# Sparse attention and a hardswish MLP on one core: filler matmuls and a new order in the first batch

## The chip, the cores and the metric

The kernel runs on one core of a Trainium2 chip. A time is the device time of one execution in microseconds (us). A core has a matrix engine (TensorE, PE in the profile; PEld is its weight load), a vector engine (VectorE, DVE), a scalar engine (ScalarE, ACT), GpSimd (POOL) and the sync engine (SyncE, SP), which here only starts transfers. Each engine works through its own instruction queue in order; semaphores tie the queues together.

## The reference

Four batches of eight heads, 768 positions of 64 dimensions. Each query sees the keys less than 16 positions away, and one summary per block of 32 keys: the maximum of k over the block stands for its keys, the mean of v for its values.

```
k_sum = k.reshape(B, H, nb, block, D).max(axis=3)
v_sum = v.reshape(B, H, nb, block, D).mean(axis=3)
scores_l = where(|i - j| < 16, scale * q k^T, -1e9)
scores_s = scale * q k_sum^T + log(block)
a = softmax(concat(scores_l, scores_s))
x = a @ concat(v, v_sum)            # heads side by side: 3072 x 512
h = x @ w_in                        # 512 x 2048
out = (h * clip(h + 3, 0, 6) / 6) @ w_out
```

Inputs are float32 in HBM; the kernel computes in bfloat16 with float32 accumulation.

## The kernel before

Heads go in pairs, four per batch, so that two heads of 64 dimensions fill 128 partitions. For batch 0 the steps are, by the names in the code:

- `K(0, p)` transposes k of a pair on PE into PSUM (line 297), copies it into the block-diagonal `kbd` (line 306; ACT one half, then DVE the other), and takes block maxima `red` and `kst` on DVE (lines 310 and 317).
- `Tq(0, p, part)` transposes q on PE (line 336) and ACT copies it to `qT` (line 337). Part 0 has the first 480 positions, part 1 the rest.
- `Sl`, called for batch 0 by `S_first`, makes the local scores `sl` (line 345), ACT their exponentials `at` (line 348), DVE the mask (line 349). `Ss` makes the scores against summaries, `ss` to `asum`, for two pairs.
- `vsum0(p)` sums v over blocks with a matmul against indicators (`vps`, line 259). After the second pair of a group, ACT copies the sums (`vs`, line 263) and two small transfers bring them into the tile `vs96` (line 266); `to_vst` spreads them on DVE.
- `vcast(p)` writes v in bfloat16 into the block-diagonal `vbd` (line 248; ACT one half, DVE the other). Its off-diagonal parts must be zero first (line 205).
- `AV(0, p, half)` accumulates outputs `num` and softmax sums `den` on PE (lines 381 to 397), ACT forms 1/den as exp(-ln den) (lines 399 and 400), DVE multiplies into `x` (line 401).
- `F1(t, ft)` multiplies a tile of 384 rows of x by a 128-column piece of `win` (line 414, tile `hp`, four matmuls), then hardswish on ACT and DVE (lines 417 and 418). It needs x of all four pairs. `F2` multiplies by `wout` (line 431).

The part for the first half of batch 0 stands under a manual schedule: the order of the calls is the order on PE, ACT and DVE. After it, `F1` and `F2` for eight row tiles run as a list, and the remaining attention work is placed in slots between them by `plan`. F1 of row tile 0 is first; `Tq(0, 0, 1)` comes after its fourth piece at the latest.

Loads: SP brings v in float32 (`vf`). GpSimd starts all others, with a cast to bfloat16: k and q of batch 0 first, then two copies named `pace` (`hold_loads`) that wait for `vs96` of the second group, and after them, in `load_weights`, w_in parts 0 and 1, the second part of q, w_in parts 2 and 3, and four parts of w_out. GpSimd is in order, so nothing is issued before the copies are done.

PSUM pools `ps_h`, `ps_o` and `ps_s` have two buffers, and `ps_n` has one each under the tags `num` and `den`. `AV` takes its two tiles in turn from `ps_o` (where `alt` is true) and `ps_n`.

Of the kernel before, what the change touches and what calls it, by code (L numbers as in the profile page):

```python
# [9 lines left out]
F32 = mybir.dt.float32  # L10
BF16 = mybir.dt.bfloat16
# [5 lines left out]
D = 64  # L17
BLK = 32
KB = 64
HALO = 15  # L20
# [12 lines left out]
def kernel(  # L33
# [9 lines left out]
    nc = tc.nc  # L43
    B, H, S, _ = q.shape
    NP = H // 2
    NB = S // BLK
    NT = S // 128
    NK = S // KB
# [93 lines left out]
    def load_w_in(c):  # L142
        w = d_ff // 4
        nc.gpsimd.dma_start(out=w_in_sb[:, :, c * w:(c + 1) * w], in_=w_in_v[:, :, c * w:(c + 1) * w])
# [34 lines left out]
    def hold_loads(src):  # L179

        nc.gpsimd.tensor_copy(pace[0:src.shape[0], 0:1], src)
# [8 lines left out]
                            channel_multiplier=-1, pattern=[[NB, 4], [0, D]])  # L190
    hmv = [hm4[:, 2 * par:2 * par + 2] for par in range(2)]
    osum = [osum4[:, 2 * par:2 * par + 2] for par in range(2)]
    obd = const.tile([128, 2, D], BF16, tag="obd", name="obd")
    hmk = const.tile([128, 2, NB], BF16, tag="hmk", name="hmk")
    half_c = const.tile([128, 1], F32, tag="half", name="half_c")
    zero = const.tile([128, 1], F32, tag="zero", name="zero")
    nc.vector.memset(zero[:], 0.0)

    def zero_off_diagonal(eng, t):
        w = t.rearrange("p n c -> p (n c)").bitcast(F32).rearrange("p (n c) -> p n c", c=64)  # L200
        for r, c in ((slice(0, 64), slice(32, 64)), (slice(64, 128), slice(0, 32))):
            if eng is nc.scalar:
                eng.copy(w[r, :, c], zero[r].unsqueeze(2).to_broadcast([64, NK, 32]))
            else:
                eng.memset(w[r, :, c], 0.0)
# [24 lines left out]
    def to_vst(g, a):  # L230
        for par in range(2):
            nc.vector.tensor_tensor(vst[2 * g + par][:], a.unsqueeze(1).to_broadcast([RS, 2, D]), hmv[par],
                                    op=ALU.mult)
# [11 lines left out]
    def vcast(p):  # L245
        for j in range(2):
            rows = slice(64 * j, 64 * j + 64)
            (nc.vector.tensor_copy if j else nc.scalar.copy)(vbd[p][rows, :, rows], vf[p][rows])


    vps, vs96 = {}, {}

    def vsum0(p):
        g, par = p // 2, p % 2
        if par == 0:
            vps[g] = ps_n.tile([128, NK, D // 2], F32, tag=("num", "den")[g], name="vps")
        for h in range(2):
            c = 2 * h + par
            nc.tensor.matmul(vps[g][32 * c:32 * c + 32], ind[:], vf[p][:, :, h * (D // 2):(h + 1) * (D // 2)],  # L259
                             start=True, stop=True)  # L260
        if par == 1:
            a = ld.tile([128, NK, D // 2], F32, tag="vr", name="vs8", bufs=2)
            nc.scalar.copy(a[:], vps[g][:])  # L263
            vs96[g] = work.tile([RS, D], F32, tag="vs96", name="vs96")
            for h in range(2):
                (nc.sync if g == 1 and h == 0 else nc.gpsimd).dma_start(
                    out=vs96[g][:, h * (D // 2):(h + 1) * (D // 2)], in_=a[64 * h:64 * h + 64:8])


# [51 lines left out]
            nc.vector.tensor_tensor(o, red[:].unsqueeze(1).to_broadcast([128, 2, NB]), hmk[:], op=ALU.mult)  # L321

    def Tq(b, p, part=None):
        pool, tag = (ps_h, "h") if b == 0 else (ps_s, "s")
        tp = pool.tile([128, S], BF16, tag=tag, name="tp")
        t, i = qb_t[b, p, part]
        if b >= NLONG:
            for s in range(NT):
                nc.tensor.transpose(tp[:, s * 128:(s + 1) * 128], t[:, s].rearrange("p h d -> p (h d)"), ident[:])
            nc.vector.tensor_copy(qT[p][:, PAD:PAD + S], tp[:])  # L330
            return
        lo, hi, n = cut(part)
        r = (hi - lo) // n
        for s in range(n):
            for j in range(2):
                nc.tensor.transpose(tp[64 * j:64 * j + 64, s * r:(s + 1) * r], t[:, 2 * i + j, s], ident[0:r, 0:r])
        nc.scalar.copy(qT[p][:, PAD + lo:PAD + hi].rearrange("p (c s) -> p c s", s=n),
                       tp[:, 0:hi - lo].rearrange("p (s c) -> p c s", s=n))
# [12 lines left out]
    def Ss(b, g, half):  # L351
        sp = ps_s.tile([128, 512], F32, tag="s", name="ss")
        for par in range(2):
            p = 2 * g + par
            nc.tensor.matmul(sp[0:RS, 0:HALF], kst[p][:], qT[p][:, PAD + half * HALF:PAD + (half + 1) * HALF],  # L355
                             start=(par == 0), stop=(par == 1))
        a = work.tile([RS, HALF], BF16, tag="asum", name="asum", bufs=4)
        nc.scalar.activation(a[:], sp[0:RS, 0:HALF], AF.Exp, scale=scl)
        asum[b, g, half] = a
# [8 lines left out]
        return res  # L368

    xt = {}  # L370

    def AV(b, p, half):
        s = 2 * b + half
        if s not in xt:
            xt[s] = xp.tile([128, NP, HALF], BF16, tag="x", name="x")
        a, asm = at[p], asum[b, p // 2, half]
        alt = b == 0 and p % 2 == half
        pool = ps_o if alt else ps_n
        num = pool.tile([128, HALF], F32, tag="o" if alt else "num", name="num")
        bl = blocks_of(half)  # L380
        nc.tensor.matmul(num[:], vst[p][:].rearrange("p h d -> p (h d)"), asm[:], start=True, stop=False)  # L381
        for i, (t, lo, hi, off) in enumerate(bl):
            nc.tensor.matmul(num[:, lo:hi], vbd[p][:, t], a[:, t, off:off + hi - lo],  # L383
                             start=False, stop=(i == len(bl) - 1))
        den = pool.tile([128, HALF], F32, tag="o" if alt else "den", name="den")
        ones = obd[:].rearrange("p h d -> p (h d)")
        nc.tensor.matmul(den[:], osum[p % 2].rearrange("p h d -> p (h d)"), asm[:], start=True, stop=False)  # L387
        t0, t1 = (0, NK // 2) if half == 0 else (NK // 2, NK)
        d3 = den[:].rearrange("p (n c) -> p n c", c=KB)
        nc.tensor.matmul(d3, ones, a[:, t0:t1, HALO:HALO + KB], start=False, stop=False)  # L390

        if half == 0:
            nc.tensor.matmul(d3[:, :, KB - HALO:], ones, a[:, 1:7, 0:HALO], start=False, stop=False)
            nc.tensor.matmul(d3[:, 1:, 0:HALO], ones, a[:, 0:5, HALO + KB:], start=False, stop=True)  # L394
        else:
            nc.tensor.matmul(d3[:, 0:5, KB - HALO:], ones, a[:, 7:12, 0:HALO], start=False, stop=False)
            nc.tensor.matmul(d3[:, :, 0:HALO], ones, a[:, 5:11, HALO + KB:], start=False, stop=True)
        lg = work.tile([128, HALF], F32, tag="lg", name="lg")
        nc.scalar.activation(lg[:], den[:], AF.Ln)  # L399
        nc.scalar.activation(lg[:], lg[:], AF.Exp, scale=-1.0)  # L400
        nc.vector.tensor_tensor(xt[s][:, p], num[:], lg[:], op=ALU.mult)  # L401
# [55 lines left out]


    def load_weights():
        for c in range(2):  # L460
            load_w_in(c)
        load_q(0, 0, 4, 1)
        for c in range(2, 4):
            load_w_in(c)
        for c in range(4):
            load_w_out(c)

    def S_first(p):
        for lo, hi in ((0, 4), (4, NK0)):
            Sl(0, p, lo, hi)  # L470

    def v_first(p):
        vsum0(p)
        vcast(p)
        if p == NP - 1:
            hold_loads(vs96[1][:, 0:1])
            hold_loads(vs96[1][:, D // 2:D // 2 + 1])
            load_weights()

    zero_rest()  # L480
    K(0, 0)
    Tq(0, 0, 0)
    v_first(0)
    for p in range(2, NP):
        zero_off_diagonal(nc.vector, vbd[p])
    S_first(0)
    v_first(1)
    K(0, 1)
    Tq(0, 1, 0)
    S_first(1)  # L490
    nc.vector.tensor_scalar_mul(osum4[:], hm4[:], float(BLK))
    K(0, 2)
    to_vst(0, vs96[0][:])
    Tq(0, 2, 0)
    Ss(0, 0, 0)
    v_first(2)
    v_first(3)
    AV(0, 0, 0)
    K(0, 3)
    Tq(0, 3, 0)  # L500
    S_first(2)
    AV(0, 1, 0)
    S_first(3)
    Ss(0, 1, 0)
    to_vst(1, vs96[1][:])
    AV(0, 2, 0)
    AV(0, 3, 0)
    start.__exit__(None, None, None)

# [56 lines left out]
                 + [(None, NTILE - 1)])  # L566
    for n, (f1, f2) in enumerate(work_list):
        for i in range(NFT):
            if f1 is not None:
                F1(f1, i, f2 is None)  # L570
            if f2 is not None:
                for j in range(3):
                    F2(f2, 3 * i + j, by_ft=f2 == 0)
            for _, f in sorted(plan.pop(16 * n + i, []), key=lambda e: e[0]):
                f()
# [31 lines left out]
```

## Time and profile before

The median of three runs is 261.19 us (261.11 to 261.37). The profiled execution has a span of 259.2 us.

| engine | busy, us | share of the span |
|---|---|---|
| PE | 238.8 | 92% |
| ACT | 167.9 | 65% |
| DVE | 155.0 | 60% |
| GpSimd | 67.4 | 26% |

| stretch, us | PE busy | DVE busy | ACT busy | DMA share |
|---|---|---|---|---|
| 0 to 5 | 0.00 | 2.86 | 4.12 | 0.62 |
| 5 to 10 | 3.57 | 2.75 | 3.77 | 1.21 |
| 10 to 15 | 2.84 | 3.52 | 2.78 | 1.24 |
| 15 to 20 | 4.31 | 4.43 | 3.71 | 0.30 |
| 20 to 25 | 4.98 | 3.15 | 3.55 | 0.14 |
| 25 to 30 | 3.42 | 2.73 | 2.17 | 1.19 |
| 30 to 35 | 4.51 | 1.11 | 2.54 | 1.24 |
| 35 to 40 | 4.29 | 3.69 | 4.44 | 1.23 |

The first column of numbers is how long PE was busy in each stretch of 5 us; the last is the mean share of time in which the 16 DMA engines had work (over 1 where packets overlap). Transfers stop between about 16 and 23 us and then run without a pause; the PE has gaps until about 36 us and few after.

### The profile page before, as it was taken

What the parts mean: (1) busy time and instruction counts of PE and PEld (TensorE: products, weight loads), DVE (VectorE), ACT (ScalarE), POOL (GpSimd) and SP (SyncE); (2) the same over time, 40 slices, a digit from 0 to 9 for tenths busy, and PEclk for the clock granted to TensorE, in tenths of its full rate; (3) what the DMA queues carried; (4) which work ended last, traced back from release to release, by engine and by line L of the source; (5) the groups of instructions that cost most, each with busy time, mean ns of one, the idle gap of its engine ahead of it and who ended that gap; (6) DMA issues with size and microseconds to landing.
All of it is one profiled execution on the core that took longest, in us unless ns stands there. A gap on an engine that the chain in (4) does not pass through costs nothing.

```text
span 259.2 us, 5011 instructions
## 1 busy us (share of the span) xinstructions
PE 238.8 (92%) x1928; PEld 139.3 (54%) x1952; DVE 155.0 (60%) x357; ACT 167.9 (65%) x326; POOL 67.4 (26%) x101
## 2 busy tenths in 40 slices
PE   1779789999999999898999999999999999999994
PEld 1336446544555656565655555666655555555553
DVE  4877266622678938999884697657544444444400
ACT  8576479733887879868676656766856655555410
POOL 7316500842893103879330400000000000000000
PEclk9999999999999999999999999999999999999999
DMA  7962999999999185999991641101011111101122
GB/s 136 197 113 33 204 204 200 149 225 214 176 188 130 57 229 73 105 82 197 168 134 41 42 61 42 43 1 43 0 40 43 40 40 43 40 0 42 43 81 81
DMA packets 62847, 25.80 MB, mean 100 GB/s; under 512 B 51280, under 2 KB 58728, under 8 KB 62824
## 3 DMA queue, kind: packets, MB, share of 16 engines
q0 software_dynamic: 52848, 17.61, 58.8%
q1 hardware_dynamic: 9976, 7.88, 9.9%
q8 instruction: 15, 0.25, 0.4%
q14 instruction: 8, 0.07, 0.1%
HBM read 31.98 MB, written 6.29 MB: 148 GB/s over the span
## 4 chain that ended last, share of the span: by engine, by line
PE 73%; DVE 11%; DMA 6%; ACT 5%; issue 2%; SPq 1%; POOL 0%; ACTq 0%
PE op L431 28%; PE hp L414 27%; DMA vf<-in_v_dram 3%; PE sl L345 3%; DVE g L418 3%; PE num L383 3%; DMA win<-in_moe_w_in_dram 2%; PE ss L355 2%; PE num L381 2%; PE den L387 2%; PE den L390 2%; DVE red L312 1%; ACT r L417 1%; DVE x L401 1%; PE vps L259 1%
## 5 line engine op out<-in xcount | busy, mean ns | idle before, releaser
L414 PE MATMUL hp<-x,win 128*128 128x384 bf16 x512 | 105.4, 328 | 2.8 <-DVE g L418 1.5
L417 ACT ACTIVATE r<-hp,half_c 128x384 f32<-128x384 f32 x128 | 73.4, 580 | 45.4 <-PE hp L414 41.9
L418 DVE SCALAR_TENSOR_TENSOR g<-r,hp 128x384 bf16<-128x384 f32 x128 | 69.7, 551 | 51.5 <-ACT r L417 51.3
L431 PE MATMUL op<-wout,g 128*128 128x512 bf16 x344 | 93.6, 379 | 1.2 <-issue 0.3
L414 PEld LDWEIGHTS <-win 128*128 128x128 bf16 x512 | 47.4, 98 | 37.8 <-issue 5.6
L431 PEld LDWEIGHTS <-g 128*128 128x128 bf16 x368 | 35.2, 98 | 30.4 <-issue 0.6
L401 DVE TENSOR_TENSOR x<-num,lg 128x384 bf16<-128x384 f32 x32 | 17.7, 554 | 26.8 <-ACT lg L400 25.2
L399 ACT ACTIVATE lg<-den 128x384 f32<-128x384 f32 x32 | 15.7, 492 | 18.8 <-PE den L394 11.2
L120 POOL DMA_DIRECT2D vbd<-in_v_dram x24 | 18.1, 768 | 36.0 <-PE num L383 23.7
L348 ACT ACTIVATE at<-sl 128x376 bf16<-128x376 f32 (+2 forms) x48 | 22.2, 488 | 4.8 <-PE sl L345 4.7
L349 DVE TENSOR_TENSOR at<-at,mask 128x376 bf16<-128x376 bf16 (+2 forms) x48 | 16.3, 348 | 3.5 <-ACT at L348 3.2
L345 PEld LDWEIGHTS <-kbd 128*128 128x128 bf16 x192 | 12.5, 103 | 9.1 <-DVE kbd L306 1.8
L400 ACT ACTIVATE lg<-lg 128x384 f32<-128x384 f32 x32 | 16.8, 526 | 0.9
L345 PE MATMUL sl<-qT,kbd 128*128 128x94 bf16 x192 | 15.5, 216 | 1.7 <-DVE kbd L306 1.6
L435 ACT COPY ot<-op 128x512 f32<-128x512 f32 x23 | 13.2, 585 | 5.9 <-PE op L431 5.7
L383 PEld LDWEIGHTS <-vbd 128*128 128x128 bf16 x224 | 13.8, 103 | 5.6 <-issue 2.4
L383 PE MATMUL num<-at,vbd 128*128 128x94 bf16 (+2 forms) x224 | 14.9, 207 | 0.0
L113 POOL DMA_DIRECT2D qb<-in_q_dram x16 | 13.6, 882 | 4.1 <-PE hp L414 2.3
L113 POOL DMA_DIRECT2D kb<-in_k_dram x16 | 13.6, 874 | 0.4 <-PE hp L414 0.4
L381 PE MATMUL num<-asum,vst 96*128 96x384 bf16 x32 | 11.2, 350 | 0.8 <-ACT vs L263 0.6
L390 PE MATMUL den<-at,obd 128*128 128x384 bf16 x32 | 11.3, 352 | 0.0
L387 PE MATMUL den<-asum,osum 96*128 96x384 bf16 x32 | 10.9, 340 | 0.0
(87 smaller groups left out, 215.3 us busy)
## 6 DMA issues: line engine op xcount, KB each, us to landing
out_dram<-ot SPq DMA_DIRECT2D x23, 256.0 KB, 2.0
vr<-in_v_dram POOLq DMA_DIRECT2D x6, 768.0 KB, 9.4
vbd<-in_v_dram POOLq DMA_DIRECT2D x24, 96.0 KB, 3.7
win<-in_moe_w_in_dram POOLq DMA_DIRECT2D x4, 512.0 KB, 9.4
wout<-in_moe_w_out_dram POOLq DMA_DIRECT2D x4, 512.0 KB, 18.0
vf<-in_v_dram SPq DMA_DIRECT2D x8, 192.0 KB, 7.5
kb<-in_k_dram POOLq DMA_DIRECT2D x16, 96.0 KB, 5.0
qb<-in_q_dram POOLq DMA_DIRECT2D x16, 96.0 KB, 4.9
```

Source lines behind the costliest of these rows:

```text
L113: nc.gpsimd.dma_start(out=t[:, :, j], in_=src[b, 2 * p + j].rearrange("(s p) d -> p s d", p=128))
L120: nc.gpsimd.dma_start(out=vall[rows, p, lo:hi, rows], in_=v[b, 2 * p + j].rearrange("(n k) d -> k n d", k=KB)[:, lo:hi])
L345: nc.tensor.matmul(sp[:, i * WIN:(i + 1) * WIN], kbd[p][:, t], qT[p][:, PAD - HALO + t * KB:PAD - HALO + t * KB + WIN], start=True, stop=True)
L348: nc.scalar.activation(a, sp[:, 0:n * WIN].rearrange("p (n c) -> p n c", c=WIN), AF.Exp, scale=scl)
L383: nc.tensor.matmul(num[:, lo:hi], vbd[p][:, t], a[:, t, off:off + hi - lo], start=False, stop=(i == len(bl) - 1))
L390: nc.tensor.matmul(d3, ones, a[:, t0:t1, HALO:HALO + KB], start=False, stop=False)
L400: nc.scalar.activation(lg[:], lg[:], AF.Exp, scale=-1.0)
L401: nc.vector.tensor_tensor(xt[s][:, p], num[:], lg[:], op=ALU.mult)
L414: nc.tensor.matmul(hp[:], w_in_sb[:, kt, ft * 128:(ft + 1) * 128], xt[t][:, kt], start=(kt == 0), stop=(kt == NP - 1))
L417: nc.scalar.activation(r[:], hp[:], AF.Relu, bias=half_c[:], scale=1.0 / 6.0)
L418: last_g[0] = nc.vector.scalar_tensor_tensor(gt[t][:, ft], r[:], 1.0, hp[:], op0=ALU.min, op1=ALU.mult)
L431: nc.tensor.matmul(op[:], gt[t][:, ft, ts * 128:(ts + 1) * 128], w_out_sb[:, ft], start=(ft == 0), stop=(ft == NFT - 1))
```

## The change

It concerns the first half of batch 0 and the loads beside it.

- **Filler.** A tile `idle` of zeros is multiplied by itself in groups (`busy`, 33 matmuls of 512 columns in all) into PSUM tiles that nobody reads. Ten stand at the head of PE's queue, the others between the steps of the prologue. They are to keep the PE occupied while it waits.
- **Order.** K and Tq of pairs 2 and 3 come ahead of the first AV; scores of all four pairs too. `vcast` of pairs 2 and 3 moves behind the scores.
- **w_in part 0** is issued by itself as soon as v is in (a `pace` copy of the last v tile), not after the sums of v. The rest of `load_weights` still waits for them.
- **Zeros** of `vbd` for pairs 2 and 3 are written by GpSimd instead of DVE.
- **PSUM.** The filler holds `den` of `ps_n` and later a buffer of `ps_h`; `vps` always uses `num`; first parts of q are transposed into `ps_o`; in the first half AV takes `ps_o` for odd pairs instead of even ones.
- **Sums of group 1** go to `vs96` through SP alone.
- **F1 of row tile 0** may not be placed ahead of the end of AV(0, 2, 0).

```diff
+    for p in range(2, NP):
+        w = vbd[p].rearrange("p n c -> p (n c)").bitcast(F32).rearrange("p (n c) -> p n c", c=64)
+        nc.gpsimd.memset(w[0:64, :, 32:64], 0.0)
+        nc.gpsimd.memset(w[64:128, :, 0:32], 0.0)
...
+    nc.vector.memset(idle[:], 0.0)
...
+    def busy(t, n):
+        for _ in range(n):
+            nc.tensor.matmul(t[:], idle[:, 0:128], idle[:], start=True, stop=True)
+    busy_n = ps_n.tile([128, 512], F32, tag="den", name="busy_n")
+    busy(busy_n, 10)
...
-                (nc.sync if g == 1 and h == 0 else nc.gpsimd).dma_start(
+                (nc.sync if g == 1 else nc.gpsimd).dma_start(
...
-        pool, tag = (ps_h, "h") if b == 0 else (ps_s, "s")
+        pool, tag = (ps_s, "s") if b else (ps_o, "o") if part == 0 else (ps_h, "h")
...
-        alt = b == 0 and p % 2 == half
+        alt = b == 0 and p % 2 == 1
...
     zero_rest()
     K(0, 0)
+    busy(busy_n, 5)
     Tq(0, 0, 0)
-    v_first(0)
-    for p in range(2, NP):
-        zero_off_diagonal(nc.vector, vbd[p])
+    vsum0(0)
+    vcast(0)
+    K(0, 1)
+    busy(busy_n, 2)
     S_first(0)
-    v_first(1)
-    K(0, 1)
     Tq(0, 1, 0)
+    busy(busy_n, 3)
+    vsum0(1)
+    vcast(1)
+    nc.vector.tensor_scalar_mul(osum4[:], hm4[:], float(BLK))
+    busy(busy_n, 2)
+    K(0, 2)
     S_first(1)
-    nc.vector.tensor_scalar_mul(osum4[:], hm4[:], float(BLK))
-    K(0, 2)
-    to_vst(0, vs96[0][:])
+    busy(busy_n, 3)
     Tq(0, 2, 0)
-    Ss(0, 0, 0)
-    v_first(2)
-    v_first(3)
-    AV(0, 0, 0)
     K(0, 3)
     Tq(0, 3, 0)
+    busy(busy_n, 3)
+    Ss(0, 0, 0)
     S_first(2)
-    AV(0, 1, 0)
+    hold_loads(vf[NP - 1][:, 0, 0:1])
+    load_w_in(0)
+    vsum0(2)
+    vsum0(3)
+    for h in range(2):
+        hold_loads(vs96[1][:, h * (D // 2):h * (D // 2) + 1])
+    load_weights()
+    to_vst(0, vs96[0][:])
+    busy_h = ps_h.tile([128, 512], F32, tag="h", name="busy_h")
     S_first(3)
     Ss(0, 1, 0)
+    vcast(2)
+    busy(busy_h, 2)
     to_vst(1, vs96[1][:])
+    AV(0, 0, 0)
+    vcast(3)
+    AV(0, 1, 0)
+    busy(busy_h, 3)
     AV(0, 2, 0)
+    first_x = last_av[0]
     AV(0, 3, 0)
```

More of the change, by code (lines that the diff above doesn't have):

```diff
@@ L196 @@
     zero = const.tile([128, 1], F32, tag="zero", name="zero")
+    idle = const.tile([128, 512], BF16, tag="idle", name="idle")
+    nc.vector.memset(idle[:], 0.0)
     nc.vector.memset(zero[:], 0.0)
+    def busy(t, n):
[3 more added lines that the diff above has]
+    busy(busy_n, 10)
     def zero_off_diagonal(eng, t):
@@ L255, in vsum0 @@
         if par == 0:
-            vps[g] = ps_n.tile([128, NK, D // 2], F32, tag=("num", "den")[g], name="vps")
+            vps[g] = ps_n.tile([128, NK, D // 2], F32, tag="num", name="vps")
         for h in range(2):
@@ L370 @@
     xt = {}
+    last_av = [None]
     def AV(b, p, half):
@@ L393, in AV @@
             nc.tensor.matmul(d3[:, :, KB - HALO:], ones, a[:, 1:7, 0:HALO], start=False, stop=False)
-            nc.tensor.matmul(d3[:, 1:, 0:HALO], ones, a[:, 0:5, HALO + KB:], start=False, stop=True)
+            last_av[0] = nc.tensor.matmul(d3[:, 1:, 0:HALO], ones, a[:, 0:5, HALO + KB:], start=False, stop=True)
         else:
@@ L459, in load_weights @@
     def load_weights():
-        for c in range(2):
-            load_w_in(c)
+        load_w_in(1)
         load_q(0, 0, 4, 1)
@@ L470, in S_first @@
             Sl(0, p, lo, hi)
[L472 to L478, printed above, removed]
     zero_rest()
     K(0, 0)
+    busy(busy_n, 5)
     Tq(0, 0, 0)
-    v_first(0)
-    for p in range(2, NP):
-        zero_off_diagonal(nc.vector, vbd[p])
+    vsum0(0)
+    vcast(0)
+    K(0, 1)
+    busy(busy_n, 2)
     S_first(0)
-    v_first(1)
-    K(0, 1)
     Tq(0, 1, 0)
+    busy(busy_n, 3)
[4 more added lines that the diff above has]
+    K(0, 2)
     S_first(1)
-    nc.vector.tensor_scalar_mul(osum4[:], hm4[:], float(BLK))
-    K(0, 2)
-    to_vst(0, vs96[0][:])
+    busy(busy_n, 3)
     Tq(0, 2, 0)
-    Ss(0, 0, 0)
-    v_first(2)
-    v_first(3)
-    AV(0, 0, 0)
     K(0, 3)
     Tq(0, 3, 0)
+    busy(busy_n, 3)
+    Ss(0, 0, 0)
     S_first(2)
-    AV(0, 1, 0)
+    hold_loads(vf[NP - 1][:, 0, 0:1])
[7 more added lines that the diff above has]
+    busy_h = ps_h.tile([128, 512], F32, tag="h", name="busy_h")
     S_first(3)
     Ss(0, 1, 0)
+    vcast(2)
+    busy(busy_h, 2)
     to_vst(1, vs96[1][:])
+    AV(0, 0, 0)
+    vcast(3)
+    AV(0, 1, 0)
+    busy(busy_h, 3)
     AV(0, 2, 0)
+    first_x = last_av[0]
     AV(0, 3, 0)
@@ L568 @@
         for i in range(NFT):
-            if f1 is not None:
+            if f1 == 0:
+                with tc.issue_after(first_x.ins):
+                    F1(0, i, True)
+            elif f1 is not None:
                 F1(f1, i, f2 is None)
```

## The prediction

> **What bounds the kernel now.** I began with the page. TensorE (PE) is busy for 92% of 259.2 us, and the chain that ended last is 73% PE, so only stretches in which PE starves, or runs slowly, can give time back. The view of who waited for whom, for PE alone, puts them at the start:
>
> ```profile
> PE tp L297 <- DMA kb<-in_k_dram: 5.3, 1, 5.3
> PE sl L345 <- DVE kbd L306: 1.6, 1, 1.6
> PE hp L414 <- DVE g L418: 1.5, 2, 1.3
> ```
>
> The first two lie before 16 us, the longest of the third at 36 us. The chain, in order of time, gives what ended last there:
>
> ```profile
> 18.02 1.48 PE vps L259 x8
> 19.52 0.48 ACT vs L263
> 20.03 1.88 DMA vs<-vs
> 22.70 5.55 DMA win<-in_moe_w_in_dram
> 28.30 1.46 PE hp L414 x4
> 33.08 1.35 PE hp L414 x7
> ```
>
> The sums of v (vps, vs) hold back the first weights (win), and these hold the first F1 matmul (hp) until 28.30; from 33.08 the chain is almost all PE. Between lie the outputs of pairs 2 and 3, and the PE timeline shows at what speed they ran:
>
> ```profile
> 24.70 0.53 PE L390 MATMUL den<-at,obd 128*128 128x384 bf16 x1
> 28.30 1.46 PE L414 MATMUL hp<-x,win 128*128 128x384 bf16 x4 [0.62 <-DMA win<-in_moe_w_in_dram]
> 33.08 1.82 PE L414 MATMUL hp<-x,win 128*128 128x384 bf16 x10 [0.39 <-DVE x L401]
> 35.67 0.43 PE L336 MATMUL tp<-ident,qb 36*64 36x36 bf16 x16 [0.77 <-DVE g L418]
> 45.50 0.33 PE L390 MATMUL den<-at,obd 128*128 128x384 bf16 x1
> ```
>
> The same den matmul takes 0.53 us at 24.7 and 0.33 at 45.5; four hp take 1.46 us at 28.3, ten take 1.82 at 33.1. PE streams at half speed until about 31.3 us. The page's PEclk row reads 9 throughout, so that row doesn't show this state; durations do. The DMA view holds the third limit:
>
> ```profile
> win<-in_moe_w_in_dram POOLq DMA_DIRECT2D x1, 512.0 KB, 5.5
> qb<-in_q_dram POOLq DMA_DIRECT2D x1, 288.0 KB, 10.1
> ```
>
> Issued at 22.70, win part 0 lands at 28.2. Part 1, issued at 23.5, lands at 30.7. Then comes the second part of q (qb, issued at 24.28) at 34.4, win part 2 at 36.5, and the rest 2.5 us apart until 49.3.
>
> [...] 4 hp start 0.32 us apart before 31.3 and 0.16 after. [...]
>
> **The change, part by part.** Everything after F1(0)'s first 16 matmuls stands in the same order on every engine as before. So the effect is how much earlier that point is reached, here measured at the first transpose of q's second part (Tq(0,0,1), 35.67 before).
>
> *Products of zeros.* 33 matmuls of 512 columns. No row shows one at the slow clock. From hp's 0.32 us for 384 columns it is 0.43 (14.1 us in all); the op rows give 0.215 at the fast clock (7.1 us). I take fast from the second or third group on: the first ten and the next five run from 1.2 us (after a memset of about 0.2 us on DVE) with only K(0,0)'s 0.8 us block between[...]. If all 15 were slow, Tq(0,0,0) would come at 8.4 instead of 7.12; nothing pays, since K(0,1) waits for its k, which lands at 9.4 (3.33 + 6.1).
>
> *Zeroing vbd of pairs 2 and 3 on GpSimd.* Takes 1.87 us from DVE (10.05 to 11.92). On GpSimd it begins at 8.84; hm, 256 columns, takes 0.31 us there, so four of 384 columns are 0.5 each[...]: done by 12.9, when nothing is due.
>
> *K, Tq of pair 3 and the casts.* In the new order PE is at K(0,2) by 13.0, when its k has landed (4.66 + 8.2 = 12.9), and at Tq(0,2) for its q at 14.4 (5.34 + 9.1). ACT from the sums of pair 1 (12.6): vs 0.4, cast 0.7, kbd 0.7, exps 0.8, qT 0.5, kbd 0.7, qT 0.5, asum 0.5: 17.4. The second scores tile of pair 2 needs the buffer that asum frees, so vps of pairs 2 and 3 runs at 17.6 to 18.4 (half of 1.48) and the copy vs ends at 19.0.
>
> *DVE* from 14.7: kbd, red, kst of pair 2 2.2, mask 0.6, the same of pair 3 2.2, mask 0.6, vst 0.5: 20.8. There AV(0,0) starts. At the fast clock one AV takes 0.9 us (44.89 to 45.75 before). ACT now sets the pace from 20.7: cast 0.8, Ln and Exp 1.0, cast 0.8, three more Ln and Exp 3.0: 26.3, with small gaps 26.7. The last x is ready 0.6 later, at **27.3**, 5.7 us ahead of 33.04. Moving the casts here costs ACT 1.7 us behind AV, but takes the same from in front of it.
>
> *win part 0 early.* Its gate is now v itself. DMA share falls at 16.2, so issue at about 16.8 and landing at 22.3; it is off the path by 5 us. *The rest of the weights* still waits for the sums of pairs 2 and 3: copy at 19.0, two issues on SP of 0.75 each instead of one on SP and one on GpSimd, 1.9 to land: 22.4, with two gate copies and the issue gap 0.7 (21.96 to 22.70 before), of which half overlaps: win part 1 issues at 22.6, 0.9 us ahead. On a then idle queue it takes 5.5: 28.1. The second part of q lands 3.7 later, as before: **31.8**.
>
> *The sum.* F1(0) runs from 27.3; sixteen matmuls and the wait for g take 2.6 as before, so PE reaches Tq(0,0,1) at 29.9 and waits there until 31.8. PE is in order, so all of F1 is queued behind it. Gain 35.67 - 31.8 = 3.9 us: 261.19 - 3.9 = **257.3**. Later loads aren't short: win part 2 lands at 33.9, due at 36.6 or later; w_out part 0 at about 39, due at 46 (49.9 before).
>
> **Rivals.**
> A (forecast, 0.55): q's second part is the new bound, 257.3. Against it: its 3.7 us may shrink on queues that are less loaded; a lead of 0.5 us either way in the sums of v moves it one for one.
> B (0.25): q lands by 29.9, [...] because the sums land early. Then the last x bounds: gain 5.7, 255.5. Against: the trace's own 3.7.
> C (0.12): PE falls back to the slow clock, in the stall before Tq(0,0,1) or between the filler groups. [...] In the second four AV of 1.85 us take the place of 0.9 and the last x slips to 31: gain about 2, 259.2.
> D (0.08), slower: the clock never rises early. 14.1 us of filler and 20.4 us of PE work before 31.3 stand in one queue from 1.2 us, with at least 1 us of waits: the last output at 36.7 instead of 32.2, less what overlaps; some 3 us lost, 264. [...]
>
> **Numbers.** A, B and C are faster by over 0.2% (0.5 us); a few of the milder forms of D end near no change. Faster 0.91, same 0.02, slower 0.07. The range takes A with its half microsecond, B down to a further 0.3, C, and leaves D out: 255.2 to 259.4.
>
> **What would show it.** In the changed profile: den L405 at 0.33 us in AV(0,0) (clock); win part 0 landed near 22; the last x of batch 0 near 27.3; tp L350 of the 36-row form waiting 1 to 2 us for DMA qb; after it the same distances as before. Wrong would be: den at 0.53; no DMA wait at that transpose (B); or a gap in the later thirds of the span that wasn't there.

## The result and the profile after

The changed kernel takes 259.21 us (four runs, 258.93 to 259.65) where the kernel before takes 261.15 (260.16 to 261.37). The ratio is 0.9935, with a 95% interval from 0.9906 to 0.9963: faster by 1.9 us, half of the forecast 3.9. Measured again later beside other kernels it was 0.9924 (0.9896 to 0.9951).

The page of the kernel after, its span, its clock row and the F1 group, and below them the F1 group on the page of before:

```profile
span 257.4 us, 5112 instructions
PEclk9999799999999999999999999999999999999999
L429 PE MATMUL hp<-x,win 128*128 128x384 bf16 x512 | 105.6, 328 | 1.7 <-DVE g L433 1.5
L414 PE MATMUL hp<-x,win 128*128 128x384 bf16 x512 | 105.4, 328 | 2.8 <-DVE g L418 1.5
```

The span is 1.8 us shorter, the F1 matmuls cost what they cost before, and the clock row now has a dip in its fifth slice. The chain that ended last, in order of time (start, length, what), answers to that of before:

```profile
18.12 1.47 PE vps L273 x8
19.59 0.02 issue
19.62 0.48 ACT vs L277
20.09 0.03 ACT at L362
20.12 4.93 DMA vs<-vs
...
25.18 0.18 POOL pace L181
...
25.86 0.76 POOL win L144
26.62 7.26 DMA qb<-in_q_dram
33.88 0.04 issue
33.93 0.43 PE tp L350 x16
```

As forecast, w_in part 0 has left the chain and q's second part has taken its place. But the transfer of the sums, vs, takes 4.93 us where it took 1.88, so the rest of the weights goes out at 25.86 and not at 22.6. Both transfers were issued by 21.54. The packets of their queue, 208 in all, move only between 23.84 and 24.70, towards the end of those of w_in part 0, which was issued at 19.26 and landed at 24.98. The PE timeline shows the other thing that the late sums did:

```profile
21.89 0.34 PE L405 MATMUL den<-at,obd 128*128 128x384 bf16 x1
26.37 0.32 PE L396 MATMUL num<-asum,vst 96*128 96x384 bf16 x1 [2.56 <-DVE x L416]
28.75 0.53 PE L405 MATMUL den<-at,obd 128*128 128x384 bf16 x1
33.93 0.43 PE L350 MATMUL tp<-ident,qb 36*64 36x36 bf16 x16 [1.45 <-DMA qb<-in_q_dram]
```

The den matmul of the first pair runs in 0.34 us: the fast clock was there. The third output then waited 2.56 us (the row names x; DVE itself was held up by `vst`, which waited 3.45 us for the sums), and the den of the fourth pair takes 0.53 again. Busy time by stretch, whose third figure from the right is the granted clock, agrees:

```profile
27.00:28.00 1.00, 1.00 (x13) 0.80 (x12) 0.56 (x1) 0.55 (x2) 1.00 (x2) 0.73 0.47 18
28.00:29.00 1.00, 1.00 (x4) 0.45 (x3) 0.51 (x1) 0.46 (x1) 1.00 (x3) 0.50 0.93 145
```

**A yardstick.** In all 16 profiles the time from the start of the fourth transpose of q's second part to the end of the span is 217.1 to 217.5 us. Nothing behind that point matters; where it stands is the result. The first row is from before, the second from after:

```profile
42.03 0.43 PE L336 MATMUL tp<-ident,qb 36*64 36x36 bf16 x16
40.09 0.43 PE L350 MATMUL tp<-ident,qb 36*64 36x36 bf16 x16
```

That is 1.94 us earlier, the measured gain. (Of it, 1.74 us stand at the first transpose already.)

### The profile page after: what moved, and what is told of

Same layout as the page of the kernel before. It is cut to its first block, busy times and chain, and to the rows that moved or that the text cites. A ratio compares the mean times of both kernels' runs of the same rounds, so it can differ in the third digit from the quotient of the medians.

```text
span 257.4 us, 5112 instructions
## 1 busy us (share of the span) xinstructions
PE 243.7 (95%) x1985; PEld 139.3 (54%) x1985; DVE 154.2 (60%) x354; ACT 167.9 (65%) x326; POOL 69.2 (27%) x105
## 4 chain that ended last, share of the span: by engine, by line
PE 75%; DVE 10%; DMA 8%; ACT 3%; issue 2%; POOL 1%; DVEq 0%; POOLq 0%; ACTq 0%
PE op L446 29%; PE hp L429 26%; PE sl L359 3%; DMA qb<-in_q_dram 3%; PE num L398 3%; DMA kb<-in_k_dram 2%; DVE g L433 2%; DMA vs<-vs 2%; PE ss L369 2%; PE num L396 2%; PE den L402 2%; DVE red L326 1%; PE den L405 1%; PE tp L350 1%; PE busy_n L208 1%
## 5 line engine op out<-in xcount | busy, mean ns | idle before, releaser
L446 PE MATMUL op<-wout,g 128*128 128x512 bf16 x368 | 98.3, 379 | 0.0
L416 DVE TENSOR_TENSOR x<-num,lg 128x384 bf16<-128x384 f32 x32 | 17.8, 555 | 22.6 <-ACT lg L415 20.8
L362 ACT ACTIVATE at<-sl 128x376 bf16<-128x376 f32 (+2 forms) x48 | 22.4, 489 | 3.2 <-PE sl L359 3.1
L398 PEld LDWEIGHTS <-vbd 128*128 128x128 bf16 x224 | 13.0, 99 | 5.8 <-issue 2.3
L359 PEld LDWEIGHTS <-kbd 128*128 128x128 bf16 x192 | 11.9, 97 | 7.6 <-issue 2.2
L359 PE MATMUL sl<-qT,kbd 128*128 128x94 bf16 x192 | 14.5, 206 | 0.4 <-ACT asum L372 0.4
L398 PE MATMUL num<-at,vbd 128*128 128x94 bf16 (+2 forms) x224 | 14.3, 201 | 0.0
L396 PE MATMUL num<-asum,vst 96*128 96x384 bf16 x32 | 10.4, 326 | 2.6 <-DVE x L416 2.6
L208 PE MATMUL busy_n<-idle 128*128 128x512 bf16 x28 | 9.6, 482 | 1.3 <-DVE ind L223 1.3
```

The lines of the kernel that those rows point to most:

```text
L359: nc.tensor.matmul(sp[:, i * WIN:(i + 1) * WIN], kbd[p][:, t], qT[p][:, PAD - HALO + t * KB:PAD - HALO + t * KB + WIN], start=True, stop=True)
L362: nc.scalar.activation(a, sp[:, 0:n * WIN].rearrange("p (n c) -> p n c", c=WIN), AF.Exp, scale=scl)
L446: nc.tensor.matmul(op[:], gt[t][:, ft, ts * 128:(ts + 1) * 128], w_out_sb[:, ft], start=(ft == 0), stop=(ft == NFT - 1))
```

## The experiments

Single runs of one kernel can differ by over 3 us (e1: 258.5 to 262.1), so a kernel is judged by its ratio to runs of before that were measured beside it. The columns on the right, from one profile each, show where a kernel stands in the chain (us). A profile can be an extreme: that of e10 is the slowest of its 19 runs, that of e2 the slowest of six, that of e3 the second fastest of eleven. In the expectations, Q names the theory of the late sums and of what they hold back, C that of TensorE's clock; the first one defines both, and a third, S.

| kernel | ratio to before, 95% interval | last x done | first, fourth transpose |
|---|---|---|---|
| before | 1 | 34.0 | 35.67, 42.03 |
| changed | 0.9935 (0.9906 to 0.9963) | 31.1 | 33.93, 40.09 |
| changed, again | 0.9924 (0.9896 to 0.9951) | 31.3 | 33.41, 39.57 |
| e1 w_in part 0 after the sums | 0.9957 (0.9935 to 0.9979) | 27.3 | 35.60, 41.56 |
| e2 q ahead of w_in part 1 | 0.9887 (0.9860 to 0.9914) | 30.9 | 32.57, 39.98 |
| e3 no filler | 0.9931 (0.9904 to 0.9958) | 29.3 | 33.05, 39.05 |
| e4 more filler | 0.9955 (0.9934 to 0.9977) | 29.9 | 33.66, 41.45 |
| e5 sums issued with part 0 | 0.9889 (0.9857 to 0.9920) | 31.0 | 33.03, 39.19 |
| e6 no gate on the sums | 0.9990 (0.9972 to 1.0008) | 34.1 | 35.70, 42.06 |
| e7 before + early part 0 | 0.9914 (0.9881 to 0.9947) | 31.7 | 33.74, 40.00 |
| e8 before + filler | 1.0013 (0.9997 to 1.0029) | 34.4 | 36.10, 42.47 |
| e10 new order alone | 0.9953 (0.9934 to 0.9973) | 28.9 | 36.42, 42.39 |
| e11 e5 without filler | 0.9943 (0.9922 to 0.9965) | 29.7 | 33.20, 40.73 |
| e12 e11, one gate | 0.9870 (0.9831 to 0.9909) | 30.7 | 33.50, 39.76 |
| e13 sums not awaited | 0.9793 (0.9763 to 0.9823) | 27.8 | 30.23, 36.49 |
| e14 e13 without filler | 0.9792 (0.9766 to 0.9818) | 29.0 | 30.78, 37.04 |

**Why the sums came late: e1, e5, e6.**

```diff
-    hold_loads(vf[NP - 1][:, 0, 0:1])
-    load_w_in(0)
 def load_weights():
+        load_w_in(0)
         load_w_in(1)
```

> The changed kernel, with w_in part 0 issued after the sums of v again (no gate on v, part 0 heads the list before part 1). Theory Q (the small transfers of the sums land late, at 25.05, because they share the DMA engines with w_in part 0; everything issued after them, q's second part above all, then sets the end of F1's fourth piece): without part 0 beside them the sums land about 1.9 us after their second issue, near 22.7. Part 0 then lands near 28.6, part 1 near 31.1, q's second part near 34.8, so its first transpose is 0.9 us later than 33.93: about 260.1 us. Theory C (the gap of 2.6 us in TensorE before the third output and the slow clock after it cost the time): the sums at 22.7 remove gap and slow clock, the transpose comes near 31.2: about 256.5. Theory S (the sums land late because both are issued by SyncE, not because of part 0): they still land near 25, part 0 only near 31, q near 37: about 262.3.

Its chain of waits:

```profile
20.25 2.33 DMA vs<-vs
22.60 0.02 POOLq L181
22.70 0.30 POOL pace L181
23.18 5.39 DMA win<-in_moe_w_in_dram
```

With no load beside them the sums are there at 22.6, 2.3 us after the second issue, though both still go through SyncE: theory S falls, and Q's 22.7 was right. The last x is done at 27.3, the very time that the prediction gave for a third output that doesn't wait. But F1 then waits 2.96 us for part 0, its first 20 matmuls take 6.1 us at the slow clock (the clock column reads 0.50 from 28 to 34 us), and the transpose comes at 35.60, later than the 34.8 of Q and far from the 31.2 of C.

```diff
-    hold_loads(vf[NP - 1][:, 0, 0:1])
-    load_w_in(0)
     vsum0(2)
     vsum0(3)
+    hold_loads(vs8[1][:, 0, 0:1])      # ACT's copy of the sums
+    load_w_in(0)
```

> The changed kernel, with the gate of w_in part 0 moved from the last v to ACT's copy of the second group's sums, so that the small transfers of the sums are issued at the same moment as part 0 and have left before its data comes. Theory Q (small transfers land late when part 0 is already moving): the sums land near 22.5 instead of 25.05, part 0 near 26, q's second part is issued near 24 and lands behind part 1 near 31.7 to 32; the third output starts near 23.7, so no gap of 2.6 us; the transpose comes near 32: about 257.4 us. If the sums are slow whenever a large load is in flight within their 2 us, they land near 26 and nothing is gained or 0.5 lost: 259.7.

Half of it came true. The first of the two transfers is there at 22.7, before most of part 0's data moves (18 GB/s from 22.0 to 22.7, 162 after it); the second, issued 0.8 us later, only at 24.7. The last x is hardly earlier than with the change, the transpose 0.4 to 0.9 us. The ratio is the better one in the middle, but its interval overlaps those of the changed kernel.

```diff
-    for h in range(2):
-        hold_loads(vs96[1][:, h * (D // 2):h * (D // 2) + 1])
     load_weights()
```

> The changed kernel without the two gate copies that wait for the sums, so that all weights and q's second part are issued in one run from about 19.3 us. Two readings of why the sums landed late. Shared engines, taken in turn: the sums still land near 25 to 26, the rest of the weights 3 us earlier, q near 28.5, and the transpose comes when DVE frees the buffer near 32.7: about 258.0. Behind everything that was queued: the sums land only after the weights, near 40 or later, the third output waits for them, and the kernel is slower than before, 270 or above.

Between the two readings. In its chain of waits the second transfer of the sums takes longest of all kernels:

```profile
20.43 7.03 DMA vs<-vs
```

So the small transfers neither pass freely nor wait for everything in line. The second of them lands 2.3 us after its issue with nothing beside it (e1), 4.4 to 4.5 with part 0 (the changed kernel and e9), 7.0 with all weights. The third output then starts at 28.56 at the slow clock (its den takes 0.53 us, and the clock column reads 0.50 from 26 to 32), and all that the earlier loads gain is lost. The gate that looked like the obstacle is needed while the sums travel this way.

**Which part brought the gain: e7, e8, e10, e3.** Each puts one part of the change on the kernel before, or takes one away. In e7 `load_w_in(0)` goes behind a `hold_loads` of the last v, and the second group's sums go to SyncE. In e8, `busy` groups of 10, 5, 3, 5 and 3 go into the old order. e10 is e1, and e3 the changed kernel, with `busy` doing nothing.

> The kernel before, with only the early issue of w_in part 0 behind the last v and both transfers of the second group's sums on SyncE, as in the change; no filler, no new order, zeros on DVE. Theory Q (the early part 0 brings the gain, and the sums that land late cost most of it): the sums land near 25, the third output starts near 25.5 and not 29.56, the last x comes near 30.5, q lands near 34: most of the change's gain, about 259.7. If the new order and the filler bring it: 261.2.

> The kernel before, with 26 products of zeros (10 at the head, the others between the first steps) and nothing else. Theory Q: w_in part 0 still lands at 28.2; the four F1 matmuls and the two outputs behind it run at the fast clock, the last x comes 1.3 us earlier, q's 34.4 lets the transpose come at most 1.2 us earlier: 260.2. Theory C (the clock is the main thing): 259.3. Worth nothing: 261.3.

> The changed kernel without any product of zeros and with w_in part 0 after the sums again: the new order of the first batch, the zeros on GpSimd and the other PSUM pools alone. Theory Q (early part 0 brings the gain): part 0 lands at about 28.4 and q's second part near 34.6, so the transpose comes 0.5 to 1 us earlier than 35.67 at most: ratio 0.997, near 260.6 us. If the order by itself brings the gain: 0.993.

> The changed kernel without any product of zeros (the tile of zeros and the PSUM tiles stay). Theory Q: TensorE is slow up to about 31 us, but it has to wait for the sums at 25 and for q at 33.9 anyway; its four outputs of 1.85 us end near 30, F1's first four pieces run partly slow and end near 34.5: about 260 us. Theory C (the clock is what the change gains by): the whole gain and more is lost, 262 or above. If the filler is worth nothing: 259.2.

The early part 0 alone (e7, with the sums on SyncE) gives 0.9914, not distinguishable from the whole change, though its third output starts at 28.0 and not at 25.5; its first transpose, at 33.74, waits for DVE, with q landed just before it, at 33.70. The filler alone (e8) gives nothing, and its removal (e3) costs nothing that these intervals show. Even e8's F1, the one place where its fast clock was to count, runs slow, four matmuls in 1.46 us as before, after PE had waited for part 0:

```profile
28.78 1.46 PE L424 MATMUL hp<-x,win 128*128 128x384 bf16 x4 [2.45 <-DMA win<-in_moe_w_in_dram]
```

Without filler (e3) the outputs run at the fast clock anyway (num and den of pair 0 in 0.33 us), against Q's expectation of a slow clock up to 31 us. The new order alone (e10) was measured at 0.9953, between its two forecasts, though its profile, the slowest of its runs, is no faster than before (42.39); in that profile F1 waits 2.87 us for part 0 and runs slow after it (20 matmuls in 5.1 us, the clock column at 0.67 and 0.50 from 30 to 34). How often it runs so isn't known from one profile. The parts don't add up: 0.9914 and 0.9953 alone, 0.9935 and 0.9924 together. That each shortens a path that another one then sets fits the profiles, but isn't shown.

**Is it the clock, or the loads: e2, e4, e11.**

```diff
 def load_weights():
+        load_q(0, 0, 4, 1)
         load_w_in(1)
-        load_q(0, 0, 4, 1)
```

> The changed kernel, with q's second part issued ahead of w_in part 1. Theory Q: q's second part lands about 31 instead of 33.88, so the first transpose waits only for the buffer that DVE frees at about 32.75; w_in part 1 lands near 33.4, before F1's fifth piece: about 258.0 us. Theory C: TensorE's own work sets the transpose, no change: 259.2. If w_in part 1 takes the place of q as the bound, between the two: 258.6.

The PE timeline of e2:

```profile
32.57 0.43 PE L350 MATMUL tp<-ident,qb 36*64 36x36 bf16 x16 [0.29 <-DVE g L433]
34.08 0.82 PE L429 MATMUL hp<-x,win 128*128 128x384 bf16 x4 [1.08 <-DMA win<-in_moe_w_in_dram]
```

The wait for q is gone and the first transpose comes at 32.6; after it F1 waits 1.08 us for w_in part 1. Up to the fourth transpose (39.98) 0.1 us is left of the gain. But this profile understates the kernel: in it k of pair 1 came late (PE waited 1.77 us for it, 0.61 in the changed kernel) and the clock fell (its row reads 7 in the third slice), and the sums were copied at 21.7 instead of 20.1, and the gate opened at 26.6 instead of 25.9. From the gate on, the pair of loads took 7.4 us where it had taken 8.0. So the bound is the pair of loads behind the gate, not q by itself. The ratio, 0.9887, is lower; its interval overlaps that of the changed kernel.

```diff
-    busy(busy_h, 3)
+    busy(busy_h, 15)
```

> The changed kernel with 15 instead of 3 products of zeros between the second and the third output, so that TensorE has no gap there and keeps its fast clock. Theory Q: the last x comes 1.5 to 2 us earlier, TensorE reaches the transpose near 30.5 and waits there for q until the same 33.9: 259.2 us, within 0.2. Theory C: the slow clock is the cause, about 257.5.

PE hardly pauses before the third output (0.16 us) and the last x is done 1.2 us sooner, but the first transpose comes at 33.66 as before, now after 2.44 us of waiting. The clock drops behind that wait instead, as its stretches show:

```profile
32.00:34.00 2.00, 0.34 (x16) 0.33 (x16) 0.87 (x2) 0.28 (x1) 0.00 (x0) 1.00 1.23 200
34.00:36.00 2.00, 2.00 (x18) 1.28 (x13) 0.00 (x0) 0.94 (x2) 0.00 (x0) 0.63 1.24 205
36.00:38.00 2.00, 2.00 (x22) 0.93 (x21) 0.96 (x2) 1.28 (x4) 0.00 (x0) 0.52 1.25 199
```

So the earlier x was worth nothing, as Q has it, and the fourth transpose is even 1.4 us later than in the changed kernel: the slow clock now falls on dense F1 work. Neither theory had foreseen that.

> The changed kernel with the gate of w_in part 0 on ACT's copy of the sums and without any product of zeros. Without filler the clock did not fall back between 26 and 31 us in earlier runs, so the last x comes near 28; but q's second part lands near 33 as it did with filler, and it sets the transpose: ratio 0.988 to 0.989, the same as with filler. If the slow clock after the gap was what still cost time there: 0.983.

A miss. The last x does come 1.2 us sooner than in e5, and the transpose stays at 33.2 as expected. But PE waits 2.12 us for q there, and the clock reads 0.70 and 0.50 in the next two stretches of 2 us; the fourth transpose is 7.5 us behind the first where it is 6.2 in the changed kernel.

This is the one pair in which the filler does show: e5 and e11 differ in nothing else, and 0.9943 lies outside e5's interval (0.9857 to 0.9920). In e5 the clock falls earlier, at the third output (den 0.46 us there, 0.53 in the fourth; the column reads 0.63 from 26 to 28 us), the last x is late, at 31.0, and PE waits only 0.72 us at the transpose. So the filler gains there by where the clock falls, and not by the fast first outputs that it was meant for. In e11 the first two outputs do run slow (den 0.53 us), and the last x is sooner all the same. This rests on one profile of each.

> As the kernel above, but the rest of the weights waits for the first small transfer of the sums alone, not for both. Theory Q: part 1 and q's second part are issued about 2 us earlier, q lands near 31; the second small transfer lands up to 2 us later, near 26.5, the last x near 29, the transpose near 31.5: ratio 0.982, about 257 us. If the second transfer is held up further by part 1 (as with no gate, 27.5): the last x near 30, transpose near 32.7, ratio 0.987.

The second outcome: the second transfer of the sums, now beside parts 0 and 1, keeps DVE waiting 3.08 us, until 25.98, the third output waits until 26.98, the last x is done at 30.7. Its ratio, 0.987, is the lowest of the kernels that await the sums; its interval overlaps those of the changed kernel. The gate opened 2.2 us earlier than there, and q, with part 0 still under way, landed only 0.4 earlier, at 33.45.

**The size of the cause: e13, e14.** Both leave out the second group's own sums: its tile gets those of the first. They measure a path and are no kernels to use.

```diff
-                    out=vs96[g][:, h * (D // 2):(h + 1) * (D // 2)], in_=a[64 * h:64 * h + 64:8])
+                    out=vs96[g][:, h * (D // 2):(h + 1) * (D // 2)], in_=vs8[0][64 * h:64 * h + 64:8])
```

> The changed kernel, but the second group's tile of sums is filled from the first group's sums, which exist at about 13.5 us (so the summary values of pairs 2 and 3 are those of pairs 0 and 1); all instructions stay. The late landing of the sums is gone: the gate for the rest of the weights opens as soon as part 0 is issued, near 20, and the third output waits for nothing from SyncE. Theory Q (the wait on the sums is the whole shortfall): q's second part lands near 28.5, the last x comes near 27.3 as forecast, the first transpose near 30 and the fourth near 36.2 instead of 40.1: ratio 0.978 to 0.980, about 255.7 us. If the slow clock, ACT's queue or the loads' own rate limit the stretch as well: 0.985 or above.

> The same without any product of zeros. With no stall in the way, TensorE's clock in the outputs is on the path: if the filler is worth what the prediction took it for, the outputs run at half speed and the last x comes 2 to 4 us later, ratio 0.988 to 0.993; if ACT sets the pace there and the clock rises by itself, 0.980 as with filler.

> The changed kernel itself once more, beside the three below, so that all four share the runs of the kernel before. Expected ratio 0.9935 as at first, within 0.002.

e13's PE timeline, at the two places that waited in the changed kernel:

```profile
23.85 0.32 PE L396 MATMUL num<-asum,vst 96*128 96x384 bf16 x1 [0.22 <-DVE x L416]
30.23 0.43 PE L350 MATMUL tp<-ident,qb 36*64 36x36 bf16 x16 [1.12 <-DMA qb<-in_q_dram]
```

With the sums out of the way the third output starts at 23.85, the last x is ready at 27.8 (27.3 in the prediction), the first transpose comes at 30.23 and the fourth at 36.49, as expected, and the ratio is 0.9793. That is a gain of 5.4 us over before, 3.5 more than the change had, and so more than the missing 2: the gate opens at 20.4 here, and the prediction had 22.6. The lead isn't passed on one for one: the gate opens 5.4 us earlier than in the changed kernel, q lands only 3.7 earlier, 9.0 us after its issue instead of 7.3. Without filler (e14) the ratio is 0.9792: the outputs are fast there too, since den reads

```profile
22.70 0.33 PE L404 MATMUL den<-at,obd 128*128 128x384 bf16 x1
```

in its first output. What raised the clock without filler isn't shown: the same steps stand ahead of the first two outputs of e11, and these ran slow. The changed kernel repeated (e9) came out as at first.

## Why the prediction was wrong

**The mechanism was right.** Part 0 left the path; the bound became q's second part; F1's first pieces stood behind it; everything later moved by nearly the same amount; no later gap appeared. The kernel fell on case A, with the wrong size.

**The step that failed** is "copy at 19.0, two issues on SP of 0.75 each instead of one on SP and one on GpSimd, 1.9 to land: 22.4". Measured: copy done at 20.1, sums landed at 25.05 (the first of the two; the second 0.2 later). Of the 2.65 us, 1.5 are the transfers. I took their 1.9 from the kernel before, where the DMA queues were empty (DMA share 0.00 from 17 to 20 us), and used it in a kernel that by its own first step has 512 KB of w_in in flight at that moment. e1 shows 1.9 and 2.3 back when part 0 is not there. The other 1.1 came before the copy. About 0.65 of it is v: I read its arrival from the DMA share that falls at 16.2 us, while the last tile landed at 17.2 even in the trace of before and at 18.6 here. So the gate of part 0 opened at 18.77 and not near 16.5, and PE had to make the sums of pairs 2 and 3 one after the other, in 1.47 us. The rest is ACT, which freed the scores buffer at 17.8 and not at 17.4. The repeat e9 shows which of these counts: there v was in at 17.8, the sums took PE 0.83 us and the copy was done at 19.5, half a microsecond behind the forecast; they landed at 24.2 and 24.8 all the same, and q only 0.5 us sooner. The transfers are the main term.

**The rest of the sum.** From landing to the next issue 0.8 us passed (I had 0.2), and q then landed 7.26 us after its issue instead of 8.4: it came 2.4 us behind part 1, not the 3.7 that I had taken over from before, where part 0 was still in flight at its issue. This second error hid part of the first. Together 2.65 + 0.6 - 1.15 = 2.1: the first transpose at 33.9 instead of 31.8, and a gain of 1.9 where 3.9 was forecast. "One for one", in the text on A, fails too, as e12 and e13 show.

**The last x**, forecast for 27.3, came at 31.1: the third output waited for the sums and the clock fell. The working followed the second group's sums only as a gate for loads, not as an input of that output; at 22.4 they would have been in time for both. It cost almost nothing here: DVE freed the buffer for the transpose at about 32.7, q came at 33.9. e13, with the wait for the sums gone, gives 27.8, so this part of the working was sound.

**Rivals.** B (255.5) didn't happen. e13 has its time, 255.6, but not its cause: PE still waits 1.12 us for q there. C did happen in part: the clock fell in the fourth output (0.73 from 27 to 28 us, 0.50 in the two after) and the last x slipped to 31, but as a consequence of the late sums, and e4 shows that mending it alone gains nothing. That C's 259.2 is the measured time is luck; the time was set by q. D was ruled out: the clock had risen by the eighth microsecond. Ten filler matmuls take 4.45 us from 1.27, the five from 6.43 take 1.50, and four of `vps` take 0.84 from 8.23, where the kernel before needed 1.50 (from 7.68). That the filler would be fast from its second or third group on was the author's estimate; what it takes to raise the clock isn't shown. The value that the prediction gave the filler, a fast clock in the outputs, is real in the trace of the changed kernel (den 0.34 us in the first output, 0.53 before), and no run shows it worth any time: of five pairs with and without filler four don't differ (before and e8, the changed kernel and e3, e1 and e10, e13 and e14), and in the fifth, e5 and e11, the difference arises elsewhere.

**Open.** Why the small transfers' packets move so late beside a large load isn't shown, only that they do. Why the clock falls after some waits of 2.1 to 3.0 us (changed kernel, e1, e4, e11) and not after others (e3 with 2.09 and 2.43, e12 with 2.81) can't be told from one profile each. Nor is it shown why q's 288 KB landed 3.7 us behind part 1 in the kernel before, where parts of 512 KB followed each other by 2.5. Sums that land near 22.4 beside an early part 0, the case that was forecast, weren't measured, nor was a way to bring the sums over without a transfer.

## What to carry to other kernels

A landing time read from an idle stretch need not hold once the change itself puts a load there: here a 12 KB transfer went from 1.9 to 4.9 us beside a 512 KB one. When a wait is removed, follow everything that its end had gated, and ask what the released transfer now travels beside. Price a transfer by its landing, not by the slice in which DMA gets quiet (here v: quiet from 16.2 us, landed at 17.2).

## What the runs showed of the hardware

- Two small SyncE transfers (12 KB each) beside large GpSimd loads: the second lands 2.3 us after its issue with nothing in flight (e1), 4.4 to 4.5 with one 512 KB load (the changed kernel and e9), 7.0 with nine loads issued in one run (e6).
- q's second part, issued right behind part 1, lands 7.2 to 7.3 us after its issue when part 0 has landed before (e9, the changed kernel), 8.7 to 10.1 when part 0 is still in flight (e1, e12, e13, before).
- The clock column of the profile reads 1.00 in the prologue of the kernel before, where a 384-column den takes 0.53 us, and 0.50 in the changed kernel when the same den takes 0.53 after having been at 0.34. Only the fall was recorded in it; the initial slow state shows in the durations alone. The stretch of before, third figure from the right:

```profile
24.00:25.00 1.00, 1.00 (x10) 0.69 (x9) 0.97 (x2) 0.68 (x3) 1.00 (x3) 1.00 0.55 22
```
